# A fused attention and two-layer kernel: weight decoding without GpSimd, the mask as a TensorE product, two token blocks side by side

## The chip, the cores and the metric

One core of one Trainium2 chip runs the kernel. The metric is the device time of one execution in microseconds, as the median of three runs: 1027.07 us before (1027.04 to 1027.49). The profiled execution has a span of 1026.5 us.

## What is computed

```python
# q, k, v: [4, 8, 576, 64]; x: 2304 tokens of 512
scores = q @ k^T / 8
# heads 0-3: 0 <= i - j < 32; heads 4-7: 0 <= i - j < 128 and (i - j) % 4 == 0
attn = softmax(where(mask, scores, -1e9)) @ v      # sums + 1e-9
x  = tokens of attn, heads side by side
xn = x / sqrt(mean(x * x) + 1e-6) * rms_g
x  = (silu(xn @ w_gate) * (xn @ w_val)) @ w_out    # 512 -> 1536 -> 512
h  = x @ w_in                                      # 512 -> 2048
out = (max(h, 0) + alpha * min(h, 0)) @ w_out2     # 2048 -> 512
```

The weights arrive as float64.

## The kernel before, in words

**Blocks and layers.** The 2304 tokens make seven blocks: 0 and 1 of 256 (the first 128 tokens of two sequences each), 2 to 5 of 384, 6 of 256. Two layers work on a block: A (gate, value and out; 12 columns of 128 hidden numbers) and B (in, PReLU and out; 16 columns). A column of A is 24 first products into an accumulator of PSUM (`mm1`, L865: hi times hi, hi times lo, lo times hi, four times, for gate and for value; in the trace `psw<-xy,wb`), tanh on ScalarE, two VectorE products, a high half on ScalarE and a low one on GpSimd (`lo`, L880), and then three second products per 128 tokens into `acc` (`mm2`, L892). `mm3` and `mm4` do the same for B. Every operand is a pair of float16 numbers, high and low. `y_out` makes B's input of A's sums, `o_out` the output.

**Weights.** A block of weights is 512 numbers a partition: 12 x 3 of A, 32 of B, 68 in all. `load_w` brings the bits, `decode_w` (L197) makes float32 of them: three steps on VectorE (L202 to L204) and one add on GpSimd (L205). `norm_w` measures them: for gate and value by products of a block with itself on TensorE (`gram`, L245, and `gram_w1`, L260), a largest entry, a diagonal that TensorE spreads over the partitions (`over_partitions`, L306, L310) and `root_scale`. That is done once for each chunk of columns in `CH = [3, 9]`: no block of a chunk is scaled before all of the chunk are decoded. `split_w` (L378) makes the halves, the high one on ScalarE; the low one on VectorE (L387), or for every third block of A and every second of B by a ScalarE copy (L384) and a GpSimd subtraction (L385).

**Attention.** A step scores a group of up to 128 queries. The first 19 groups are float32 products (`f_turn`, `f_score`, `f_turn_p`, `f_value`), transposed by TensorE (L595, L621), the later 33 float16 pairs. `softmax` (L534) takes scores from PSUM, scales and masks them on VectorE by a minimum with a mask tile (L541), finds the maxima and lets ScalarE do exponentials. `a_norm` (L691, L693) divides by the root mean square, `a_xT` (L705) transposes x into a block's `xy`.

**Order.** The program issues the work of a slot (a column of a layer and block): due attention steps (`take`), decoding (`pump`), splits, first products, then second products of an earlier column (`flush`). The layers come in the order A0 A1 A2 B0 B1 B2 A3 B3 A4 B4 A5 B5, with A6 ahead of B5. In A0 all second products come after the twelve columns (`LAG0 = 12`). `N0 = 8` blocks of weights are decoded during block 0's attention; the rest of A by the end of A0, and B's during A1 and A2. A scheduler then sets the order of each engine's queue, in which the engine runs it. PSUM's eight banks are three for `acc` (`ps_a`) and five for all else (`ps_w`, in the trace `psw`). `L92` is the helper that records every product.

Of the kernel before, what the change touches and what calls it, by code (L numbers as in the profile page):

```python
# [19 lines left out]
NEG = -1.0e9  # L20
BIG = 3.0e38
# [8 lines left out]
def kernel(  # L30
# [27 lines left out]
    NXY = 3  # L58
# [4 lines left out]
    ps_a = ctx.enter_context(tc.tile_pool(name="ps_a", bufs=3, space=PSUM))  # L63
    ps_w = ctx.enter_context(tc.tile_pool(name="ps_w", bufs=5, space=PSUM))
    dram = ctx.enter_context(tc.tile_pool(name="dram", bufs=1, space=DRAM))

# [5 lines left out]
    xy = [const.tile([128, 2, KD, TMAX], F16, name=f"xy{i}") for i in range(NXY)]  # L72
# [5 lines left out]
    eps = const.tile([128, 3], BF16, name="eps")  # L78
    mhalf = const.tile([128, 1], F32, name="mhalf")
    m_norm = const.tile([96, 128], BF16, name="m_norm")  # L80
    m_tail = const.tile([32, 96], BF16, name="m_tail")
    m_spp = const.tile([128, 128], BF16, name="m_spp")
# [42 lines left out]
    def constants():  # L125
# [5 lines left out]
        nc.vector.memset(ones_1, 1.0)  # L131
        nc.vector.memset(eps, 1e-30)
        nc.gpsimd.memset(qkhl, 0.0)
        nc.vector.memset(mhalf, -0.5)
        for m in (m_spp, m_norm, m_tail):
            nc.vector.memset(m, BIG)
        band(m_spp, 128, 128, 0, -31, 0)
        # m_spd: 0 <= p - c and p % 4 == c % 4
# [8 lines left out]
        nc.vector.tensor_scalar(m_spd, same, BIG, NEG, ALU.mult, ALU.add)  # L147
        band(m_spd, 128, 128, 0, -127, 0)
        band(m_norm, 96, 128, 0, 1, 32)
# [9 lines left out]
    # A block (512 numbers a partition) is two slots of 2 KB as it comes, one as float32 and  # L159
    # one as hi | lo.  # L160
# [12 lines left out]
    def one_slot():  # L173
        # the one that has been free for the longest
# [22 lines left out]
    def decode_w(b):  # L197
# [6 lines left out]
        nc.vector.tensor_scalar(r[:, :, 0], r[:, :, 0], 29, None, ALU.logical_shift_right)  # L204
        nc.gpsimd.tensor_tensor(w, w, r[:, :, 0], ALU.add)  # L205
# [39 lines left out]
    def gram(blocks, sums, dst):  # L245
        # blocks of [k, f]: each one's own columns, or the sums over all of them
# [35 lines left out]
    def norm_w(b):  # L282
# [7 lines left out]
        else:  # L290
            # sums of squares, on the engine that waits least then
# [3 lines left out]
            if b == NBLK - 1:  # L295
# [3 lines left out]
                mm(g[:, 0:2], ones_1, eps[:, 0:2], True, False)  # L299
# [6 lines left out]
    def over_partitions(src, n, dst):  # L306
        # the largest of the partitions' src[:, i], on every partition
# [7 lines left out]
    def root_scale(p, sg, rc):  # L315
        # p: bounds of squares. sg = 2^n with sqrt(p) sg < 2^15; rc = 1 / sg
# [6 lines left out]
    # scales: gate and val of each chunk, out of each, in2, out2  # L323
# [9 lines left out]
    def scale_g():  # L333
        # sx with |x / rms * g| sx < 2^15, as |x / rms| <= sqrt(512)
# [8 lines left out]
    def scale_wo():  # L343
        # S with |out| S / (gate's scale * val's) < 2^15 in every chunk
# [12 lines left out]
        # what the last products carry: 2^-60 / (1/sx^2 * 1/S * 1/si * 1/sp)  # L357
# [33 lines left out]
    # The first 128 tokens of the sequences, the next 384 of each, and what is left of them.  # L391
# [61 lines left out]
    # the groups up to this one are float32 products  # L453
# [32 lines left out]
    def a_split_hi(i):  # L486
# [4 lines left out]
        mm(ps[:, 0:3], ones_1, eps, True, False)  # L491
# [4 lines left out]
        # sc: 0:3 the scales of q, k, v; 3:6 their inverses by 2^50; 6 that of the scores  # L496
# [36 lines left out]

    def softmax(g, scores, scale):  # L534
        # scores: (in PSUM, their heads); leaves exp(s - max) in g["s"] and its sums in g["dn"]
        nq, nk = g["nq"], g["nk"]
        s = g["s"]
        sv = s[:nq, :, :nk]
# [29 lines left out]
    # The first 128 tokens of the sequences: float32 products, as the tensor engine waits for  # L568
    # weights then; the tiles are slots of the weights that are not yet there.
# [34 lines left out]
    def f_score(i):  # L604
        g = groups[i]
        nq, nk, qk = g["nq"], g["nk"], g["qk"]
        # products of different rows of the array go to different banks
        pss = [psw()[:, 0:256].rearrange("p (h c) -> p h c", h=2) for _ in range(2)]
        for h in range(HH):
            p0 = 64 * (h % 2)  # L610
            mm(pss[h % 2][:nq, h // 2, :nk], qk[p0:p0 + 64, h // 2, :nq], qk[p0:p0 + 64, 2 + h // 2, :nk], True, True)
# [26 lines left out]
    def a_score(i):  # L638
# [3 lines left out]
        ps = psw().rearrange("p (h c) -> p h c", h=HH)  # L642
# [496 lines left out]
```

## Time and profile before

| | us |
|---|---|
| median of three runs (1027.04 to 1027.49) | 1027.07 |
| span of the profiled execution | 1026.5 |
| TensorE busy (6270 products) | 937.2, 91% |
| VectorE busy (1396 instructions) | 575.6, 56% |
| ScalarE busy (1604) | 559.9, 55% |
| GpSimd busy (394) | 377.8, 37% |

Shares are of the span of the profiled execution. The page cuts the span into 40 slices of 25.7 us; digits are tenths of a slice that the engine was busy, and PEclk the TensorE clock that was granted, in tenths of 2.4 GHz:

```profile
PE   5454879988889989999999999999999999999997
DVE  5999986787888766564445575434352111331111
POOL 3564645345534454533232333322142211122222
PEclk9676889999899999999999999999999999999999
```

PE is TensorE, PEld its loading of the stationary operand, DVE VectorE, ACT ScalarE, POOL GpSimd, SP SyncE.

### The profile page before, as it was taken

To read this page: it belongs to the slowest core of one execution; us is meant where nothing else is said; L and a number is where in the kernel's file an instruction comes from. 1 tells how busy PE (TensorE), PEld (TensorE's weight loads), DVE (VectorE), ACT (ScalarE), POOL (GpSimd) and SP (SyncE) were. 2 spreads that over 40 slices of the span, in tenths; PEclk is the share of its full clock that TensorE was granted. 3 is DMA by queue.
4 is the path that set the end of the run, shared out by engine and by line. 5 is a ranking of instruction groups with operands and counts; after the bars stand their busy time and mean duration, and the time that the engine had idled before them with its cause. 6 is when DMAs were issued, how large, how long until landed. Compare 5 with 4: busy or idle time off the path is not lost.

```text
span 1026.5 us, 17830 instructions
## 1 busy us (share of the span) xinstructions
PE 937.2 (91%) x6270; PEld 583.3 (57%) x6270; DVE 575.6 (56%) x1396; ACT 559.9 (55%) x1604; POOL 377.8 (37%) x394
## 2 busy tenths in 40 slices
PE   5454879988889989999999999999999999999997
PEld 3444765566545656665555555555555555765564
DVE  5999986787888766564445575434352111331111
ACT  3142657554669988777655677644454312333343
POOL 3564645345534454533232333322142211122222
PEclk9676889999899999999999999999999999999999
DMA  9991323643454354344344353331120000101000
GB/s 255 299 338 45 101 72 102 160 118 102 146 110 96 64 96 93 80 97 99 67 106 64 85 117 80 79 84 38 38 43 6 29 16 1 32 1 21 1 31 21
DMA packets 191608, 88.06 MB, mean 86 GB/s; under 512 B 176800, under 2 KB 180384, under 8 KB 191520
## 3 DMA queue, kind: packets, MB, share of 16 engines
q1 hardware_dynamic: 188896, 82.22, 33.0%
q10 hardware_dynamic: 2624, 4.72, 1.4%
q8 instruction: 49, 0.80, 0.3%
q14 instruction: 39, 0.32, 0.1%
HBM read 55.32 MB, written 6.55 MB: 60 GB/s over the span
## 4 chain that ended last, share of the span: by engine, by line
PE 68%; DVE 18%; DMA 6%; ACT 4%; issue 2%; POOL 1%; SPq 1%; ACTq 0%; DVEq 0%; POOLq 0%
PE psw L92 40%; PE acc L92 27%; DVE wb L203 3%; DVE wb L204 3%; DVE wb L202 2%; DMA wb<-in_moe_w_in_dram 2%; DVE wb L387 2%; DMA wb<-in_moe_w_out_dram 1%; DVE wb L693 1%; DVE wb L541 1%; DMA rkv<-in_v_dram 1%; DMA qkT<-qkhl 1%; DVE dn L556 1%; ACT wb L549 1%; POOL wb L205 1%
## 5 line engine op out<-in xcount | busy, mean ns | idle before, releaser
L92 PE MATMUL psw<-xy,wb 128*128 128x384 f16 (+1 forms) x3360 | 530.3, 307 | 5.2 <-DVE t L875 2.7
L92 PEld LDWEIGHTS <-wb 128*128 128x128 f16 (+1 forms) x4014 | 390.4, 100 | 247.5 <-issue 13.4
L92 PE MATMUL acc<-wb,hl 128*128 128x512 f16 x1002 | 246.2, 381 | 4.9 <-ACT hl L877 1.2
L932 DVE SCALAR_TENSOR_TENSOR p<-m,nal,p 128x384 f32<-128x384 f32 (+1 forms) x112 | 71.4, 638 | 166.6 <-ACT p L931 166.0
L92 PEld LDWEIGHTS <-hl 128*128 128x128 f16 x1002 | 96.0, 98 | 98.8 <-issue 3.4
L205 POOL TENSOR_TENSOR wb<-wb 128x512 int32<-128x512 int32 x68 | 100.3, 1482 | 94.5 <-DVE wb L203 61.8
L92 PE MATMUL acc<-wb 128*128 128x512 f16 x510 | 124.0, 379 | 0.7 <-ACT wb L934 0.6
L883 POOL TENSOR_TENSOR hl<-p,hl 128x384 f16<-128x384 f32 (+1 forms) x74 | 61.3, 828 | 116.4 <-ACT hl L934 103.9
L883 POOL TENSOR_TENSOR hl<-t,hl 128x384 f16<-128x384 f32 (+1 forms) x56 | 51.1, 912 | 129.6 <-ACT hl L877 129.6
L874 DVE SCALAR_TENSOR_TENSOR t<-t,psw 128x384 f32<-128x384 f32 (+1 forms) x84 | 41.2, 490 | 79.9 <-ACT t L873 79.7
L930 ACT ACTIVATE m<-psw 128x384 f32<-128x384 f32 (+1 forms) x112 | 48.6, 434 | 65.9 <-PE psw L92 65.1
L873 ACT ACTIVATE t<-psw,tsc 128x384 f32<-128x384 f32 (+1 forms) x84 | 44.1, 525 | 71.9 <-PE psw L92 62.7
L92 PE MATMUL psw<-wb 128*128 128x128 bf16 (+6 forms) x448 | 57.3, 301 | 10.7 <-POOL wb L205 8.4
L659 POOL TENSOR_TENSOR phl<-s,phl 96x512 f16<-96x512 f32 (+2 forms) x33 | 36.8, 1114 | 70.0 <-ACT phl L653 40.5
L382 ACT ACTIVATE wb<-wb,wsg 128x512 f16<-128x512 f32 x68 | 46.6, 711 | 27.3 <-DVE wrc L321 18.7
L875 DVE SCALAR_TENSOR_TENSOR t<-t,psw 128x384 f32<-128x384 f32 (+1 forms) x84 | 41.2, 490 | 27.8 <-PE psw L92 26.5
L549 ACT ACTIVATE s<-s,mx 96x128 f32<-96x128 f32 (+2 forms) x132 | 50.1, 381 | 10.9 <-DVE mx L546 10.7
L883 POOL TENSOR_TENSOR wb<-p,wb 128x384 f16<-128x384 f32 (+1 forms) x38 | 32.0, 842 | 63.5 <-ACT wb L934 57.5
L203 DVE SCALAR_TENSOR_TENSOR wb<-wb 128x512 int32<-128x512 int32 x68 | 54.7, 810 | 0.2
L883 POOL TENSOR_TENSOR wb<-t,wb 128x256 f16<-128x256 f32 (+1 forms) x28 | 24.1, 861 | 80.2 <-ACT wb L877 72.1
L877 ACT ACTIVATE hl<-t 128x384 f16<-128x384 f32 (+1 forms) x56 | 26.8, 479 | 44.4 <-DVE t L875 44.4
L934 ACT ACTIVATE hl<-p 128x384 f16<-128x384 f32 (+1 forms) x74 | 34.6, 467 | 28.9 <-DVE p L932 28.8
(160 smaller groups left out, 1154.2 us busy)
## 6 DMA issues: line engine op xcount, KB each, us to landing
wb<-in_moe_w_out_dram SPq DMA_DIRECT2D x28, 512.0 KB, 4.4
wb<-in_moe_w_in_dram SPq DMA_DIRECT2D x16, 512.0 KB, 3.6
wb<-in_moe_w_gate_dram SPq DMA_DIRECT2D x12, 512.0 KB, 7.7
wb<-in_moe_w_val_dram SPq DMA_DIRECT2D x12, 512.0 KB, 7.3
out_dram<-o ACTq DMA_DIRECT2D x16, 256.0 KB, 2.5
rkv<-in_k_dram SPq DMA_DIRECT2D x23, 128.0 KB, 2.7
rkv<-in_v_dram SPq DMA_DIRECT2D x23, 128.0 KB, 2.8
rq<-in_q_dram SPq DMA_DIRECT2D x23, 96.0 KB, 2.1
```

The lines of the kernel that those rows point to most:

```text
L92: nc.tensor.matmul(o, a, b, start=start, stop=stop)
L203: nc.vector.scalar_tensor_tensor(w, r[:, :, 1], -0x40000000, w, ALU.bitwise_and, ALU.bitwise_or)
L205: nc.gpsimd.tensor_tensor(w, w, r[:, :, 0], ALU.add)
L382: nc.scalar.activation(half(b, 0), dec(b), ACTF.Copy, scale=wsg[:, s:s + 1])
L549: nc.scalar.activation(s[:nq, h, :nk], s[:nq, h, :nk], ACTF.Exp, bias=mx[:nq, 1, h:h + 1], accum_out=g["dn"][:nq, h])
L659: nc.gpsimd.tensor_tensor(phl[:nq, 1, :, :nk], g["s"][:nq, :, :nk], phl[:nq, 0, :, :nk], ALU.subtract)
L873: nc.scalar.activation(t[:, :T], pg[:, :T], ACTF.Tanh, scale=tsc[:, chunk(c):chunk(c) + 1])
L874: nc.vector.scalar_tensor_tensor(t[:, :T], t[:, :T], 1.0, pg[:, :T], ALU.add, ALU.mult)
L875: nc.vector.scalar_tensor_tensor(t[:, :T], t[:, :T], 2.0 ** -46, pv[:, :T], ALU.mult, ALU.mult)
L883: nc.gpsimd.tensor_tensor(a[:, 1, :T], t[:, :T], a[:, 0, :T], ALU.subtract)
L930: nc.scalar.activation(m[:, :T], ps[:, :T], ACTF.Relu, scale=-(2.0 ** -15))
L932: nc.vector.scalar_tensor_tensor(p[:, :T], m[:, :T], nal[:, c:c + 1], p[:, :T], ALU.mult, ALU.add)
```

## The change

- Decoding ends on VectorE: the add becomes a shift and an or in one instruction (two inputs); GpSimd has no part in it.
- All low halves of weights are made on VectorE.
- The mask (0 or -1e38, in bfloat16) is a product: the identity times the mask, the first into the bank of the scores. VectorE's minimum goes; maxima and exponentials read PSUM.
- `CH` is `[2, 3, 3, 4]`, `N0` is 4.
- A0 and A1 alternate by column, block 1 two columns behind; both blocks' second products stand behind all of the first ones. Then come A2, A3, B0 and B1 alternating, B2, A4, B3, A5, B4, A6, B5, B6. B's weights are decoded in A2 and A3, 1.75 blocks a slot, the rest ahead of B0.
- x of blocks 0, 1 and 4 share one buffer, 2 and 5, 3 and 6 one each.
- One pool of eight banks in place of three and five.

```diff
-        nc.vector.tensor_scalar(r[:, :, 0], r[:, :, 0], 29, None, ALU.logical_shift_right)
-        nc.gpsimd.tensor_tensor(w, w, r[:, :, 0], ALU.add)
+        nc.vector.scalar_tensor_tensor(w, r[:, :, 0], 29, w, ALU.logical_shift_right, ALU.bitwise_or)
...
-    CH = [3, 9]
+    CH = [2, 3, 3, 4]
...
-        if n_split[0] % (LO1 if b < NW1 else LO2) == 0:
-            nc.scalar.activation(dec(b), dec(b), ACTF.Copy, scale=wsg[:, s:s + 1])
-            nc.gpsimd.tensor_tensor(half(b, 1), dec(b), half(b, 0), ALU.subtract)
-        else:
-            nc.vector.scalar_tensor_tensor(half(b, 1), dec(b), wsg[:, s:s + 1], half(b, 0), ALU.mult, ALU.subtract)
+        nc.vector.scalar_tensor_tensor(half(b, 1), dec(b), wsg[:, s:s + 1], half(b, 0), ALU.mult, ALU.subtract)
...
+    def masked(g, ps, n):
+        nq, nk = g["nq"], g["nk"]
+        mm(ps[:nq, 0:n, :nk], identb[:nq, :nq],
+           g["mask"][:nq, :nk].unsqueeze(1).to_broadcast([nq, n, nk]), True, False)
...
         for ps, hs in scores:
-            n = len(range(HH)[hs])
-            nc.vector.scalar_tensor_tensor(
-                s[:nq, hs, :nk], ps[:nq, :, :nk], scale,
-                g["mask"][:nq, :nk].unsqueeze(1).to_broadcast([nq, n, nk]), ALU.mult, ALU.min)
+            nc.vector.tensor_reduce(mx[:nq, 0, hs], ps[:nq, :, :nk], axis=AX.X, op=ALU.max)
+        nc.vector.tensor_scalar(mx[:nq, 1], mx[:nq, 0], scale, -1.0, ALU.mult, ALU.mult)
...
-    LAG0 = 12
-    N0 = 8
+    SKEW = 2
+    N0 = 4
...
+    for c in range(C1 + SKEW):
+        slots += [("A", j, c - SKEW * j) for j in (0, 1) if 0 <= c - SKEW * j < C1]
+    for p, j in (("A", 2), ("A", 3), ("B", 0), ("B", 2), ("A", 4), ("B", 3), ("A", 5), ("B", 4), ("A", 6), ("B", 5), ("B", 6)):
+        if (p, j) == ("B", 0):
+            slots += [("B", i, c) for c in range(C2) for i in (0, 1)]
...
+        if kind == "A" and j < 2:
+            if last and j == 1:
+                flush("A", 0, 0)
+                flush("A", 1, 0)
+        else:
+            flush(kind, j, 0 if last else LAG)
```

TensorE's queue before, from the first scale's diagonal to the first layer product (`psw<-xy`; 128x64 products are attention values, those of L705 transposes of x):

```order
L92 LDWEIGHTS ones_79
L92 MATMUL psw<-diag,ones_79 128x256
L92 MATMUL psw<-wb 128x64 x8
L705 MATMUL psw<-ident,wb 128x128 x8
L595 MATMUL psw<-ident,wb 128x128 x8
L92 LDWEIGHTS wb
L92 MATMUL psw<-xy_73,wb 128x256
```

The same place in the change (L623 are transposes of attention weights, L708 those of x; 128x128 products of `wb` behind a load are gram products, 15 more of which and the diagonal follow):

```order
L623 MATMUL psw<-ident,wb 128x128 x13
L96 MATMUL psw<-wb 128x64 x4
L623 MATMUL psw<-ident,wb 128x128 x3
L96 MATMUL psw<-wb 128x64 x12
L708 MATMUL psw<-ident,wb 128x128 x8
L96 LDWEIGHTS wb
L96 MATMUL psw<-wb 128x128
```

The value products and the transposes have moved from behind the diagonal to ahead of the gram products.

VectorE's queue before, around the second tile's normalization (L693):

```order
L691 TENSOR_SCALAR ms<-ms 128x1
L256 TENSOR_REDUCE nrm<-psw 128x1
L203 SCALAR_TENSOR_TENSOR wb<-wb 128x512
L256 TENSOR_REDUCE nrm<-psw 128x1
L310 TENSOR_SCALAR diag<-ident,nrm 128x128
L202 TENSOR_SCALAR wb<-wb 128x512
L204 TENSOR_SCALAR wb<-wb 128x512
L363 TENSOR_REDUCE big<-al 128x1
L373 TENSOR_SCALAR nal<-al 128x16
L693 SCALAR_TENSOR_TENSOR wb<-wb,ms,gs 128x512
```

In the change, around the first (L696; L208 to L210 are the decoding):

```order
L694 TENSOR_SCALAR ms<-ms 128x1
L561 TENSOR_TENSOR wb<-psw,dn 128x256
L209 SCALAR_TENSOR_TENSOR wb<-wb 128x512
L363 TENSOR_SCALAR k_101<-xsc 128x1
L208 TENSOR_SCALAR wb<-wb 128x512
L696 SCALAR_TENSOR_TENSOR wb<-wb,ms,gs 128x512
L210 SCALAR_TENSOR_TENSOR wb<-wb 128x512
```

No reduction of a gram product (L256) and no diagonal (L310) stands ahead of the normalization any more; decoding steps still do.

## Rows read from the trace of the kernel before

**Rows 1.** Stretches: span, busy time of PE, PEld, DVE, ACT, POOL; PEclk, DMA share, GB/s.

```profile
0.00:63.50 63.50, 28.10 (x138) 21.80 (x139) 52.07 (x119) 19.50 (x55) 31.77 (x38) 0.78 1.00 293
63.50:269.00 205.50, 167.23 (x1231) 123.48 (x1230) 176.96 (x372) 108.44 (x326) 105.47 (x87) 0.88 0.40 119
269.00:430.00 161.00, 151.62 (x1101) 95.03 (x1100) 117.91 (x293) 133.71 (x392) 75.67 (x80) 1.00 0.45 92
430.00:1026.40 596.40, 590.20 (x3805) 342.96 (x3803) 228.63 (x615) 298.24 (x831) 164.86 (x191) 1.00 0.23 50
```

**Rows 2.** Chain of waits, 840 to 1026: start us, us, engine, tile, line, count.

```profile
844.43 3.90 PE psw L92 x24
848.33 1.94 PE acc L92 x9
...
888.57 2.29 PE psw L92 x21
892.49 2.29 PE psw L92 x21
```

**Rows 3.** Two stretches, first products (tile xy): PE, DVE, ACT, clock, DMA.

```profile
63.50:269.00 205.50, 86.52 (x594) 4.23 (x7) 3.12 (x6) 0.88 0.40 119
269.00:430.00 161.00, 90.79 (x613) 0.00 (x0) 0.00 (x0) 1.00 0.45 92
```

**Rows 4.** The same stretches, second products (tile acc).

```profile
63.50:269.00 205.50, 34.82 (x138) 1.47 (x2) 2.62 (x6) 0.88 0.40 119
269.00:430.00 161.00, 66.41 (x264) 3.62 (x5) 7.83 (x17) 1.00 0.45 92
```

**Rows 5.** Stretches, VectorE's masking alone (L541): DVE, PEclk, DMA share, GB/s.

```profile
63.50:269.00 205.50, 11.53 (x30) 0.88 0.40 119
269.00:430.00 161.00, 7.10 (x10) 1.00 0.45 92
430.00:1026.40 596.40, 15.94 (x23) 1.00 0.23 50
```

**Rows 6.** PE's timeline, 25 to 64: start us, us, operation [idle before, releaser].

```profile
30.60 0.41 PE L621 MATMUL psw<-ident,wb 128*128 128x128 f32 x1
...
40.73 0.39 PE L92 MATMUL psw<-diag,ones 128*128 128x256 bf16 x1 [8.36 <-DVE diag L310]
40.91 3.56 PE L92 MATMUL psw<-wb 128*128 128x64 f32 x16
...
60.92 1.09 PE L705 MATMUL psw<-ident,wb 128*128 128x128 f32 x4 [15.59 <-DVE wb L693]
```

**Rows 7.** DVE's timeline, 44 to 64.

```profile
45.23 1.50 DVE L204 TENSOR_SCALAR wb<-wb 128x512 int32<-128x512 int32 x1
...
50.82 0.68 DVE L707 TENSOR_TENSOR xy<-psw,xy 128x512 f16<-128x512 f32 x1
...
59.13 1.64 DVE L693 SCALAR_TENSOR_TENSOR wb<-wb,ms,gs 128x512 f32<-128x512 f32 x1
```

**Rows 8.** PE's timeline, 76 to 97.

```profile
81.62 4.45 PE L92 MATMUL psw<-wb 128*128 128x128 bf16 x40 [6.16 <-POOL wb L205]
...
94.83 0.37 PE L92 MATMUL psw<-diag,ones 128*128 128x256 bf16 x1 [6.11 <-DVE diag L310]
```

**Rows 9.** Decoding by line: duration ns min/median/max, first to last start us.

```profile
L203 DVE SCALAR_TENSOR_TENSOR wb<-wb x68: 654/678/1777, 5.3 to 295.0; 128x512 int32<-128x512 int32 x68
...
L204 DVE TENSOR_SCALAR wb<-wb x68: 408/420/1498, 5.0 to 294.1; 128x512 int32<-128x512 int32 x68
...
L205 POOL TENSOR_TENSOR wb<-wb x68: 1272/1292/2961, 6.1 to 295.7; 128x512 int32<-128x512 int32 x68
```

**Rows 10.** POOL's timeline, 44 to 48.

```profile
44.72 3.15 POOL L205 TENSOR_TENSOR wb<-wb 128x512 int32<-128x512 int32 x2 [1.63 <-DVE big L365]
```

**Rows 11.** Low halves on VectorE (L387): DVE, PEclk, DMA share, GB/s.

```profile
269.00:430.00 161.00, 13.39 (x16) 1.00 0.45 92
```

**Rows 12.** Low halves on GpSimd (L385): POOL, PEclk, DMA share, GB/s.

```profile
269.00:430.00 161.00, 18.85 (x16) 1.00 0.45 92
```

More of the change, by code (lines that the diff above doesn't have):

```diff
@@ L19 @@
 EXPO = 0x7F800000
-NEG = -1.0e9
-BIG = 3.0e38
+NEG = -1.0e38
 @with_exitstack
@@ L71 @@
     wbi = wb.bitcast(I32)
-    xy = [const.tile([128, 2, KD, TMAX], F16, name=f"xy{i}") for i in range(NXY)]
+    xy0 = const.tile([128, 2 * 2 * KD * 256], F16, name="xy0")
+    xyl = [const.tile([128, 2, KD, TMAX], F16, name=f"xy{i}") for i in (1, 2)]
+    xy = [xy0[:, i * 2 * KD * 256:(i + 1) * 2 * KD * 256].rearrange("p (a k t) -> p a k t", a=2, k=KD) for i in range(2)]
+    xy += xyl + [xy0[:, 0:2 * KD * TMAX].rearrange("p (a k t) -> p a k t", a=2, k=KD)] + xyl
+    after_b = {4: (0, 1), 5: (2,), 6: (3,)}
     gs = const.tile([128, DM], F32, name="gs")
@@ L146, in constants @@
         mm(same, et.rearrange("p a c -> p (a c)"), et.rearrange("p a c -> p (a c)"), True, True)
-        nc.vector.tensor_scalar(m_spd, same, BIG, NEG, ALU.mult, ALU.add)
+        nc.vector.tensor_scalar(m_spd, same, -NEG, NEG, ALU.mult, ALU.add)
         band(m_spd, 128, 128, 0, -127, 0)
-        band(m_norm, 96, 128, 0, 1, 32)
+        band(m_band, 128, 160, 0, 1, 32)
         for r in range(2):
@@ L830, in hl_take @@
         T = ncols(j % 100)
-        if j == 0:
-            h_at[c] = one_slot()
-            t = wb16[:, h_at[c] * 1024:h_at[c] * 1024 + 2 * T].rearrange("p (a t) -> p a t", a=2)
+        if j < 2:
+            if c not in h_at:
+                h_at[c] = [one_slot(), 2]
+            o = h_at[c][0] * 1024 + j * 512
+            t = wb16[:, o:o + 2 * T].rearrange("p (a t) -> p a t", a=2)
         else:
@@ L844, in hl_give @@
         t = ah_at.pop((j, c))
-        if j == 0 and c in h_at:
-            give(h_at.pop(c))
+        if j < 2:
+            h_at[c][1] -= 1
+            if h_at[c][1] == 0:
+                give(h_at[c][0])
         else:
@@ L887, in accumulate @@
             if first:
-                acc[n] = ps_a.tile([128, DM], F32, tag="acc", name="acc")
+                acc[j, n] = ps_w.tile([128, DM], F32, tag="w", name="acc")
             for u, (l, m) in enumerate(((0, 0), (0, 1), (1, 0))):
-                mm(acc[n], a[:, l, n * 128:(n + 1) * 128], half(b, m), first and u == 0, last and u == 2)
+                mm(acc[j, n], a[:, l, n * 128:(n + 1) * 128], half(b, m), first and u == 0, last and u == 2)
     def mm2(j, c):
@@ L946, in o_out @@
             o = wk.tile([128, DM], F32, tag="st", bufs=2, name="o")
-            nc.scalar.activation(o, acc[n], ACTF.Copy, scale=rc[:, n:n + 1])
+            nc.scalar.activation(o, acc[j, n], ACTF.Copy, scale=rc[:, n:n + 1])
             col = 0
@@ L957 @@
     LAG = 1
-    LAG0 = 12
-    N0 = 8
+    SKEW = 2
+    N0 = 4
     START = (-1, 0, 1, -1, 2, -1, 3, -1)
     RAW = 10
-    PUMP = (1.5, 1.5, 2.0)
-    SP0, SP1 = 10, 6
-    LOOK = 4
-    phases = [(p, j) for p in "AB" for j in range(3)]
-    for j in range(3, NJ - 2):
-        phases += [("A", j), ("B", j)]
-    phases += [("A", NJ - 2), ("A", NJ - 1), ("B", NJ - 2), ("B", NJ - 1)]
-    ahead = {j + 1 for n, (p, j) in enumerate(phases) if p == "A" and phases[n + 1:n + 3] == [("B", j), ("A", j + 1)]}
-    slots = []
-    for p, j in phases:
-        slots += [(p, j, c) for c in range(C1 if p == "A" else C2)][LOOK if p == "A" and j in ahead else 0:]
-        if p == "A" and j + 1 in ahead:
-            slots += [("A", j + 1, c) for c in range(LOOK)]
+    PUMP = 1.75
+    slots = []
+    for c in range(C1 + SKEW):
[4 more added lines that the diff above has]
+        else:
+            slots += [(p, j, c) for c in range(C1 if p == "A" else C2)]
     def dur(s):
@@ L986 @@
     need = [(n + 1, start_of[j] - 8.0) for n, (_, j) in enumerate(steps) if j]
+    steps_of = {j: n + 1 for n, (_, j) in enumerate(steps) if j is not None}
     done_b = set()
-    state = dict(done=0, clock=0.0, credit=0.0, spare=12)
+    state = dict(done=0, clock=0.0, credit=0.0, pump=0.0, spare=6)
     def take(d):
@@ L994, in take @@
         got = []
-        while steps and state["credit"] >= 1.0 and len(got) < 2:
+        while steps and state["credit"] >= 1.0 and len(got) < 3:
             j = steps[0][1]
-            if j is not None and j >= NXY and j - NXY not in done_b:
+            if j is not None and not done_b.issuperset(after_b.get(j, ())):
                 break
@@ L1004, in first_step @@
     def first_step():
-        steps.popleft()[0]()
+        f, j = steps.popleft()
+        assert j is None or done_b.issuperset(after_b.get(j, ()))
+        f()
         state["done"] += 1
@@ L1034, in pump_to @@
             pump(1)
+            assert loaded or n_done[0] >= n, (n_done, n, sum(free), len(later))
     pend = {}
@@ L1078 @@
             f()
+        while kind == "A" and state["done"] < steps_of[j]:
+            first_step()
         if (kind, j) == ("A", 0):
@@ L1082 @@
                 split_w(b)
-        if kind == "A" and j < 3:
-            state["spare"] = (SP0, SP1, 3)[j]
-            state["pump"] = state.get("pump", 0.0) + PUMP[j]
+        if kind == "A" and j in (2, 3):
+            state["spare"] = 6 if j == 2 else 3
+            state["pump"] += PUMP
             pump(int(state["pump"]))
             state["pump"] -= int(state["pump"])
-        while (kind, j, c) == ("B", 0, 0) and (loaded or later):
-            pump(1)
+        if (kind, j, c) == ("B", 0, 0):
+            state["spare"] = 2
+            pump_to(NBLK)
         if (kind, j) == ("B", 0):
@@ L1100 @@
         last = c == (C1 if kind == "A" else C2) - 1
-        early_one = kind == "A" and j in ahead and c < LOOK
-        flush(kind, j, 0 if last else LAG0 if (kind, j) == ("A", 0) else LOOK if early_one else LAG)
+        if kind == "A" and j < 2:
+            if last and j == 1:
+                flush("A", 0, 0)
+                flush("A", 1, 0)
+        else:
+            flush(kind, j, 0 if last else LAG)
 _INS = ['q', 'k', 'v', 'moe_w_gate', 'moe_w_val', 'moe_w_out', 'moe_rms_g', 'moe2_w_in', 'moe2_w_out', 'moe2_alpha']
```

65 lines of the change are left out of this document (32 added, 33 removed).

## The prediction, made before the changed kernel ran

> **What bounds the kernel now.** I read the cut into stretches first, then the chain of waits, then TensorE's timeline where it stands. The four stretches [rows 1] end where the first layer product starts (63.5 us), where blocks 0 and 1 are through the first layer but for a few products (269), and where as many products are done as the change has before its block 0 enters the second layer (430). After 430 TensorE is busy for 590.2 of 596.4 us at full clock: there it is the bound. Before 269 it is busy for 28.1 of 63.5 and 167.2 of 205.5 us, at a granted clock of 0.78 and 0.88 of 2.4 GHz, while VectorE is busy for 52.1 and 177.0: the loss sits there.
>
> The layer products have a fixed price at full clock [rows 2]: 24 of 384 columns take 3.90 us, nine of 512 take 1.94 (0.216 each), and one column of a 256 block takes 892.49 - 888.57 = 3.92, of which six of 512 are 1.29 and 24 of 256 the other 2.63 (0.110 each). A block of 384 costs 12 x (3.90 + 1.94) + 16 x (3.90 / 2 + 1.94) = 132.3, one of 256 costs 12 x 3.92 + 16 x (2.63 / 2 + 1.29) = 88.6; four and three of them make **795 us**, in either kernel. The other 231 us of the span of 1026.5 are attention, scales, waiting and slow clock. By stretch:
> - 0 to 63.5: no layer product.
> - 63.5 to 269 (205.5): 594 products of mostly 256 columns [rows 3] and 138 of 512 [rows 4], some 95 us; idle 205.5 - 167.2 = 38; the clock's missing 12% of the busy time, 20; so attention and scales 52, for 15 groups (30 mask instructions, two for a group there [rows 5]).
> - 269 to 430 (161): idle 9.4; 613 products [rows 3], by the program 270 of them with 384 columns, and 264 of 512 [rows 4] make 270 x 0.1625 + 343 x 0.110 + 264 x 0.216 = 138.6, I take 139; so 12.6 for ten groups, 1.26 each.
> - 430 to the end (596.4): products 795 - 95 - 139 = 561; idle 6.2; 29 for 23 groups [rows 5], again 1.26 each.
>
> **The change, part by part.** *Start.* The first product waits for x of block 0. The last transpose of the attention weights ends at 31.0, but TensorE then does gram products and stands 8.36 us at the diagonal of their scale, with 16 value products queued behind it; and it stands 15.59 us for the second tile's normalization on VectorE, whose queue is full of decoding [rows 6]. In the change the value products and the transposes stand ahead of most gram products, and four decodes instead of eight are asked for first. The values can then start at 31 and take 3.6 [rows 6]; normalization is, for each of two tiles, 1.64 for the scaling and 0.68 for each of two copies [rows 7], 1.09 for transposes [rows 6] and about 0.4 for the square's sum, 4.5: 9 in all, so 44. Gram, diagonal, scale and first splits come to 4 more: **48**. Bounds: 43 if these lie wholly beside that, 58 if the second tile waits as long as 10 us.
>
> *Blocks 0 and 1 in the first layer* (the change has their attention and first products side by side). Products 95, attention and scales of the same 15 groups 52, two groups more 2.5, and 30 mask products: by the rate above 0.11 each, so 3; the nearest row for one that starts alone is 0.37 [rows 8], so at most 11, and a gain is excluded, as they are added to TensorE. That is 152. What is lost besides? Before, 38 + 20 = 58. The largest piece is the second chunk of nine columns: between 75 and 95 TensorE waits 6.16 and 6.11 us [rows 8] for 18 decodes and then for their scale. With chunks of 2, 3, 3 and 4 columns the wait is cut in pieces, between which the second block's products stand; I keep three scale chains of 6 us (18), 10 for the second block's attention, which now comes due as early as the first columns, and 5 at half clock. Bounds: 10, and all 58. 152 + 33 = 185, so **233** instead of 269.
>
> Is VectorE the bound there? A decode now is 0.42 + 0.68 + 0.68 us there (medians [rows 9]) instead of 0.42 + 0.68 + 0.42 and a GpSimd add of 1.29. But VectorE's instructions are held up: a single-input step of 0.42 takes 1.50 [rows 7] beside a GpSimd add that runs from 44.72 [rows 10]. Pricing the stretch's 372 VectorE instructions at the shortest common duration of their forms (as 0.42 and 0.68) gives 127 us, against 177.0 busy [rows 1]: 50 more, beside 105.5 us of GpSimd, 0.47 for each. For the change the same count is 117, beside 16 us of GpSimd: 117 + 7 = 124 of 185. Not the bound.
>
> *Blocks 2 and 3, with the second layer's weights.* The change decodes 30 blocks here instead of 6, and VectorE takes the low halves of all 27 splits, where of 32 it had 16 [rows 11] and ScalarE and GpSimd 16 [rows 12]; 15 groups run instead of ten. TensorE: products 140, 15 groups at 1.26, 19, and a 512-column mask product for each at 0.216, 3: 162. VectorE: the count is 85 before, against 117.9 busy beside 75.7 of GpSimd [rows 1], 0.44 for each. In the change it is 139. GpSimd loses six adds (7.7) and 18.9 of splits [rows 12], which leaves 49, and five groups' subtractions come on top, some 52: 139 + 0.44 x 52 = 162. Two engines equally full cannot hide each other: I give 16 us of idle TensorE instead of 9.4. 178, so **411** instead of 430. Nothing hides VectorE's work here: if it is late, the splits are, and TensorE waits. Bounds: 165 (3 of idle) and 188.
>
> *From there.* Products 795 - 95 - 140 = 560, 16 groups instead of 23 at 1.26 and 0.216 for the mask, 24, idle 6.2: 590 instead of 596.4. The eight-bank pool I cost at nothing: in this stretch TensorE's 6.2 us of idle are all that banks could cost, and where blocks 0 and 1 sum in four banks, four are left for the products; at worst that doubles the 6. ScalarE loses 28 copies; with 133.7 busy of 161 [rows 1] it has no more to do. 48 + 185 + 178 + 590 = 1001, and with the 0.6 us around the span (the median is 1027.07, the profiled span 1026.5) **1002 us**.
>
> **The rivals.** *VectorE bounds blocks 2 and 3* (slower). If each of GpSimd's 52 us cost VectorE a whole one, it needs 139 + 52 = 191; and if it then reaches only the share of its busiest long stretch, 177.0 of 205.5 or 86% [rows 1], the stretch is 222 and the kernel 1002 + 44 = 1046. It decides once VectorE needs over 176: the stretch then passes 205, and the kernel 1029. The rows before come to 0.44 and 0.47 of that price. For: all decoding and all low halves stand in one queue. Against: most of GpSimd's share is gone. Chance 0.13.
> The Trainium skill, "SBUF — State Buffer", section "Who interferes with whom", says that a VectorE instruction with two SBUF inputs, or in a two-port mode, and one of GpSimd exclude each other, the second waiting for the whole of the first. By that rule the price could be this rival's; the 1.50 us step agrees with it, the averages bear out half.
> *The waits only move.* The side-by-side blocks wait for the same weights and lose 45 to 58, not 33; with masks at 0.37 the stretch is at most 152 + 8 + 58 = 218, the kernel 1002 + 33 = 1035, and 1014 to 1027 with cheap masks. For: TensorE's queue has a fixed order, and four scale chains in it instead of two. Against: each chain has other products ahead of it. Chance 0.12.
> *It packs.* Start at 44, losses of 10, third stretch 165: 1002 - 4 - 23 - 13 = 962. For: at each chain TensorE has another block's products. Against: VectorE is 162 of the 165. Chance 0.13.
> That the change doesn't do what it says its order excludes: no add on GpSimd and no mask on VectorE is left.
>
> **How the numbers follow.** The forecast has 0.62 and, with its bounds partly used, 975 to 1024. The range of 970 to 1030 leaves out most of the packed case and of VectorE's, and the end of the moved waits. A difference under 0.2% (2 us) can't be told from none. Faster: 0.61 of the forecast, 0.13 packed, 0.04 of the moved waits: 0.78. Same: 0.01, 0.05 of the moved waits and 0.01 of VectorE's: 0.07. Slower: 0.03 and 0.12: 0.15.
>
> **What would show it.** The first layer product at 43 to 58; blocks 0 and 1 through the first layer near 233, block 0's entry into the second layer near 411; decode steps at their medians, with none over 1 us except beside a GpSimd subtraction; idle TensorE between these two marks 3 to 26 us. I am wrong if TensorE idles for more than 60 us between the first product and 411, if its last 590 us change, or if the mask products cost more than 15 us together.

## The result, and the profile after

The change made the kernel **slower: 1036.86 us** (median of four runs, 1035.23 to 1038.1) against 1027.05 (four runs), 1.0% by these medians; the ratio that goes with the runs is 1.0104 (95% interval 1.0087 to 1.0122). The prediction was 1002, 970 to 1030. The profiled execution has a span of 1035.7 us, 9.2 more than before.

The stretches of the change, cut at the same work as [rows 1] (first layer product; blocks 0 and 1 through layer A; as many products as stand ahead of B0; the end), with the same columns:

```profile
0.00:53.50 53.50, 31.95 (x143) 23.88 (x143) 33.11 (x97) 17.09 (x56) 7.49 (x19) 1.00 1.06 287
53.50:232.90 179.40, 159.75 (x1290) 120.39 (x1291) 143.68 (x382) 103.39 (x329) 31.53 (x32) 0.90 0.46 124
232.90:424.90 192.00, 170.14 (x1158) 97.06 (x1157) 154.10 (x407) 142.76 (x413) 56.53 (x51) 0.96 0.58 134
424.90:1035.70 610.80, 590.18 (x3756) 346.88 (x3754) 197.26 (x509) 290.33 (x780) 161.98 (x195) 0.99 0.19 40
```

| stretch | before | predicted | after |
|---|---|---|---|
| to the first layer product | 63.5 | 48 | 53.5 |
| blocks 0 and 1 in layer A | 205.5 | 185 | 179.4 |
| the products of A2 and A3, or as many | 161 | 178 | 192.0 |
| the rest | 596.4 | 590 | 610.8 |

Up to 233 us the numbers came as forecast and 36 us were won. Then 31 were lost in 192 us, 17 of them forecast: TensorE idles there for 192.0 - 170.1 = 21.9 us, and is busy for 170.1 us at a granted clock of 0.96 where 162 were forecast. Another 14 were lost in the rest, where TensorE now idles for 610.8 - 590.2 = 20.6 us instead of 6.2.

TensorE's timeline at the start (start, us, operation, idle time before it and its releaser), for [rows 6]:

```profile
36.91 1.12 PE L708 MATMUL psw<-ident,wb 128*128 128x128 f32 x4 [2.24 <-DVE wb L696]
40.14 1.09 PE L708 MATMUL psw<-ident,wb 128*128 128x128 f32 x4 [2.11 <-DVE wb L696]
...
47.93 0.37 PE L96 MATMUL psw<-diag,ones 128*128 128x256 bf16 x1 [5.00 <-DVE diag L315]
...
53.49 0.28 PE L96 MATMUL psw<-xy,wb 128*128 128x256 f16 x1 [2.63 <-ACT wb L383]
```

The 15.59 us for the second tile are 2.11, and x is transposed at 41.2, ahead of the sum's 44. From there to the first layer product it takes 12.3 us where the sum had 4: the diagonal still costs 5.00 and a split 2.63. Runs whose edits lie behind blocks 0 and 1 reach the first layer product at 50.3 to 54.5, so that some 3 us of the difference are not the change's own. The last step of decoding, for [rows 9] (ns min/median/max, first to last start):

```profile
L210 DVE SCALAR_TENSOR_TENSOR wb<-wb x68: 649/680/1518, 5.8 to 338.1; 128x512 int32<-128x512 int32 x68
```

Decoding ends at 338 us instead of 296: the second layer's weights moved to where A2 runs.

### The profile page after: what moved, and what is told of

It reads as the page before. It is cut to its first block, busy times and chain, and to the rows that moved or that the text cites. A ratio compares the mean times of both kernels' runs of the same rounds, so it can differ in the third digit from the quotient of the medians.

```text
span 1035.7 us, 17720 instructions
## 1 busy us (share of the span) xinstructions
PE 952.0 (92%) x6343; PEld 588.2 (57%) x6343; DVE 528.2 (51%) x1391; ACT 553.6 (53%) x1576; POOL 257.5 (25%) x296
## 4 chain that ended last, share of the span: by engine, by line
PE 61%; DVE 11%; DMA 6%; ACT 5%; issue 3%; SPq 1%; POOL 1%; ACTq 0%; DVEq 0%; POOLq 0%
PE psw L96 35%; PE acc L96 25%; DVE wb L209 2%; DMA qkT<-qkhl 1%; DVE wb L210 1%; DMA rkv<-in_k_dram 1%; ACT s L548 1%; DVE wb L208 1%; DMA rq<-in_q_dram 1%; DMA xy<-yhl 1%; DVE t L882 1%; DVE mx L543 1%; DVE t L883 1%; DVE wb L384 1%; DMA pT<-phl 1%
## 5 line engine op out<-in xcount | busy, mean ns | idle before, releaser
L96 PE MATMUL psw<-xy,wb 128*128 128x384 f16 (+1 forms) x3360 | 518.7, 305 | 4.4 <-ACT wb L383 2.6
L96 PEld LDWEIGHTS <-wb 128*128 128x128 f16 (+1 forms) x3975 | 382.5, 99 | 232.0 <-issue 10.8
L96 PE MATMUL acc<-wb,hl 128*128 128x512 f16 x1041 | 258.3, 387 | 19.8 <-ACT hl L942 11.3
L96 PE MATMUL acc<-wb 128*128 128x512 f16 x471 | 113.7, 385 | 5.0 <-ACT wb L383 3.1
L891 POOL TENSOR_TENSOR hl<-p,hl 128x384 f16<-128x384 f32 (+1 forms) x84 | 67.6, 805 | 168.8 <-ACT hl L942 161.2
L891 POOL TENSOR_TENSOR wb<-t,wb 128x256 f16<-128x256 f32 (+1 forms) x36 | 32.8, 911 | 164.5 <-ACT wb L885 154.3
L548 ACT ACTIVATE s<-psw,mx,sc 96x128 f32<-96x128 f32 (+2 forms) x132 | 56.8, 435 | 12.1 <-DVE mx L544 8.3
L384 DVE SCALAR_TENSOR_TENSOR wb<-wb,wsg 128x512 f16<-128x512 f32 x68 | 51.7, 782 | 4.2 <-ACT wb L383 3.4
L939 ACT ACTIVATE p<-psw 128x384 f32<-128x384 f32 (+1 forms) x112 | 49.0, 437 | 0.0
L210 DVE SCALAR_TENSOR_TENSOR wb<-wb 128x512 int32<-128x512 int32 x68 | 47.9, 714 | 0.2
L209 DVE SCALAR_TENSOR_TENSOR wb<-wb 128x512 int32<-128x512 int32 x68 | 47.0, 701 | 0.2
```

The costliest lines, as they stand in the source:

```text
L96: nc.tensor.matmul(o, a, b, start=start, stop=stop)
L209: nc.vector.scalar_tensor_tensor(w, r[:, :, 1], -0x40000000, w, ALU.bitwise_and, ALU.bitwise_or)
L210: nc.vector.scalar_tensor_tensor(w, r[:, :, 0], 29, w, ALU.logical_shift_right, ALU.bitwise_or)
L548: nc.scalar.activation(s[:nq, h, :nk], ps[:nq, n, :nk], ACTF.Exp, bias=mx[:nq, 1, h:h + 1], scale=scale, accum_out=g["dn"][:nq, h])
L891: nc.gpsimd.tensor_tensor(a[:, 1, :T], t[:, :T], a[:, 0, :T], ALU.subtract)
L939: nc.scalar.activation(p[:, :T], ps[:, :T], ACTF.Relu, scale=2.0 ** -15)
```

## The experiments

Labels that begin with b_ are the kernel before with parts of the change, a_ the change with parts undone. The first theory put the loss on the order of the blocks (attention held back until B0 and B1 are done), the rival on the parts.

### Parts put into the kernel before

**b_no_gpsimd** (decoding and low halves).

```diff
-        nc.vector.tensor_scalar(r[:, :, 0], r[:, :, 0], 29, None, ALU.logical_shift_right)
-        nc.gpsimd.tensor_tensor(w, w, r[:, :, 0], ALU.add)
+        nc.vector.scalar_tensor_tensor(w, r[:, :, 0], 29, w, ALU.logical_shift_right, ALU.bitwise_or)
...
-        if n_split[0] % (LO1 if b < NW1 else LO2) == 0:
-            nc.scalar.activation(dec(b), dec(b), ACTF.Copy, scale=wsg[:, s:s + 1])
-            nc.gpsimd.tensor_tensor(half(b, 1), dec(b), half(b, 0), ALU.subtract)
-        else:
-            nc.vector.scalar_tensor_tensor(half(b, 1), dec(b), wsg[:, s:s + 1], half(b, 0), ALU.mult, ALU.subtract)
+        nc.vector.scalar_tensor_tensor(half(b, 1), dec(b), wsg[:, s:s + 1], half(b, 0), ALU.mult, ALU.subtract)
```

> The kernel before, with two parts of the change: the last step of decoding and all low halves of weights on VectorE, GpSimd in neither. Theory O (the order of the blocks costs the time: attention of block 4 is held until both B0 and B1 are done and then comes in a bunch): these two parts are good by themselves, since the 118 us of GpSimd adds and subtractions that go had cost VectorE 0.45 us each, 53, against some 40 us of added VectorE work: 1010 to 1022 us. Theory P (the parts cost it, not the order): VectorE, full from 25 to 130 us, gets more work: 1030 to 1045.

**b_decode_dve** (the first hunk of that diff alone).

> The kernel before with the last step of decoding on VectorE alone, low halves as before. If each us of GpSimd costs VectorE 0.45 us until 270, the 100 us of adds that go give 45 back and 68 instructions of 0.68 for 0.42 take 18: some 27 of the 37 us: 996 to 1005. If the low halves were the larger part: 1010 to 1022.

Measured: **989.37 us**, ratio 0.9641 (0.9626 to 0.9655), more than either theory gave, and 990.94 for decoding alone. The first two stretches of b_no_gpsimd, cut at the same work:

```profile
0.00:53.20 53.20, 28.01 (x139) 21.77 (x139) 40.33 (x111) 18.40 (x53) 8.37 (x21) 0.86 1.02 283
53.20:234.50 181.30, 156.23 (x1228) 118.90 (x1227) 162.79 (x392) 101.08 (x314) 26.29 (x29) 0.90 0.49 153
```

Blocks 0 and 1 are through at 234.5 us **in the old order, with the old chunks and masks**; the whole change needs 232.9. So taking GpSimd out is worth the whole gain up to there; what the chunks and the order do besides cancels, as the runs below show. The same step undone inside the change gives it back, **a_add_on_gpsimd** (the first hunk the other way round):

> The changed kernel with the last step of decoding back on GpSimd. In the kernel before, this part alone was worth 35 us, until 235 us of the span. If the parts add: 1060 to 1078 us, and the first layer of blocks 0 and 1 ends near 265 instead of 233. If blocks side by side hide GpSimd's adds: 1036 to 1050.

1075.63 us, 38.8 above the change: this part adds, as expected. But blocks 0 and 1 end at 248 us, not near 265, and 22 of the 38.8 stand in block 2 (112.7 us instead of 90.9), where the second layer's weights are now decoded.

**b_mask** (the `masked` products and the new `softmax`, as in the diff of the change, alone) and **b_one_pool**:

```diff
-    ps_a = ctx.enter_context(tc.tile_pool(name="ps_a", bufs=3, space=PSUM))
-    ps_w = ctx.enter_context(tc.tile_pool(name="ps_w", bufs=5, space=PSUM))
+    ps_w = ctx.enter_context(tc.tile_pool(name="ps_w", bufs=8, space=PSUM))
...
-                acc[n] = ps_a.tile([128, DM], F32, tag="acc", name="acc")
+                acc[n] = ps_w.tile([128, DM], F32, tag="w", name="acc")
```

> The kernel before with the mask as a product alone. Theory O: VectorE loses 37.6 us of masking, of which a part lay on the way before 270, TensorE gets 71 products of 0.1 to 0.35 us; 1018 to 1030 us. Theory P: a product that heads every score and exponentials that hold a bank of PSUM for longer: 1032 to 1042.

> The kernel before with one pool of eight banks alone. Theory O: nothing, 1024 to 1030 us, as TensorE idles for 6 us in all after 430. Theory P: sums and products that take each other's banks make TensorE wait behind ScalarE's and VectorE's reading: 1032 or more, with idle time in the last 600 us.

1034.07 us, ratio 1.0085 (1.0065 to 1.0104), and 1036.48, 1.0107 (1.009 to 1.0124): both are losses by themselves, 8 and 10 us. For the mask, one stretch of equal products (200 to 600 us of them) before:

```profile
431.50:824.90 393.40, 392.92 (x2555) 221.58 (x2554) 184.61 (x509) 230.19 (x673) 123.30 (x137) 1.00 0.32 69
```

and with it:

```profile
428.40:829.10 400.70, 398.42 (x2583) 224.46 (x2582) 170.78 (x486) 235.39 (x673) 123.36 (x137) 1.00 0.33 67
```

The stretch grew by 7.3 us. TensorE has 5.5 more to do for 23 groups, 0.24 each, and VectorE 13.8 less, which nobody waits for there; ahead of the stretch 3.1 are won (428.4 against 431.5). Why one pool costs is open: in its profiled run, the fastest of the four, the loss is spread, 1.5 us ahead of 433 and 2.6 from there to 829.

**b_no_gpsimd_chunks**, which is b_no_gpsimd with

```diff
-    CH = [3, 9]
+    CH = [2, 3, 3, 4]
...
-    N0 = 8
+    N0 = 4
```

and **all_but_order**, the same with the edits of b_mask and b_one_pool too.

> The kernel before with decoding and low halves on VectorE and the chunks of 2, 3, 3 and 4 (four blocks decoded first). The parts measured so far add up to 1007 without the chunks, against 1012 with them: if parts add, the chunks are worth -3 to +7: 986 to 997 us. If they save the waits for the nine-column chunk, as the prediction had it: 970 to 982.

> The kernel before with decoding and low halves on VectorE, mask as a product, chunks of 2, 3, 3 and 4 and one pool, in the old order of blocks: all of the change but the order. Theory S: 989 + 8 + 10 = 1007, with the chunks unknown within 6: 1000 to 1014 us, 10 groups of attention done between the end of layer A for blocks 0 and 1 and the point of 234.6 us of products, in 160 to 170 us instead of 192. Theory I: 1025 to 1040.

1002.48 us, so the chunks **lose 13** where the prediction counted on them, and 1012.43: mask and pool together cost 10 here, not 18, so these two do not add. In b_no_gpsimd_chunks TensorE meets the last chunk's gram products in the middle of A0:

```profile
138.46 1.87 PE L92 MATMUL psw<-wb 128*128 128x128 bf16 x12 [3.70 <-DVE wb L204]
143.76 1.21 PE L92 MATMUL psw<-wb 128*128 128x128 bf16 x8 [3.43 <-DVE wb L204]
```

The wait for decoding is not gone, it stands later; b_no_gpsimd has none there.

### The order behind A1

**side_by_side_only** is b_no_gpsimd_chunks with A0 and A1 side by side, **a_old_tail** is all_but_order with the same edit, which also decodes the second layer's weights in A2 alone (not shown):

```diff
-    phases = [(p, j) for p in "AB" for j in range(3)]
+    phases = [("A", 2)] + [("B", j) for j in range(3)]
...
+    for c in range(C1 + SKEW):
+        slots += [("A", j, c - SKEW * j) for j in (0, 1) if 0 <= c - SKEW * j < C1]
```

> The kernel before with decoding and low halves on VectorE, the chunks, and blocks 0 and 1 side by side in layer A, but the old order behind them (A2 B0 B1 B2 A3 B3 ...), the mask on VectorE and the old pools. Theory S: side by side is no loss, the order behind A1 is: 975 to 992 us. Theory I: side by side itself makes VectorE late: 995 to 1015.

> The changed kernel with the old order behind A1 (A2 B0 B1 B2 A3 B3 A4 B4 A5 A6 B5 B6, four columns of the next A ahead), and nothing else changed: B's weights are decoded in A2 alone. Theory S: the 30 us of the order come back but for what A2 loses to decoding: 1002 to 1018 us. Theory I: 1028 or more.

1013.16 and 1015.82 us. A0 beside A1 is no gain: it costs 10.7 us in the first pair (1002.48 without it), inside the range of the theory against it, and 3.4 in the second (1012.43 without it; the runs scatter by that much). But it does gain where the prediction looked for it. These are the times, in us, at which layer products worth 95 us (blocks 0 and 1 in layer A) and 235 us have started, each priced as in the prediction:

| layer products | b_no_gpsimd | b_no_gpsimd_chunks | side_by_side_only | all_but_order | a_old_tail | change |
|---|---|---|---|---|---|---|
| 95 us | 234.0 | 242.4 | 234.0 | 238.2 | 227.0 | 232.2 |
| 235 us | 391.6 | 403.9 | 415.8 | 400.7 | 404.3 | 424.5 |

Side by side wins 8 and 11 us up to the first mark, about what the chunks lose there, and loses 20 and 15 up to the second. Of the 68 loads of weights, 21 (side_by_side_only) and 14 (a_old_tail) come behind the first mark, instead of 4 and 5.

The order behind A1, with what goes with it (the buffers of x, one for `pT` where there were two, the pace of decoding), costs 1036.86 - 1015.82 = 21. Where? **a_a3_later** moves A3, and decodes the second layer's weights in A2 alone:

```diff
-    for p, j in (("A", 2), ("A", 3), ("B", 0), ("B", 2), ("A", 4), ("B", 3), ("A", 5), ("B", 4), ("A", 6), ("B", 5), ("B", 6)):
+    for p, j in (("A", 2), ("B", 0), ("A", 3), ("B", 2), ("A", 4), ("B", 3), ("A", 5), ("B", 4), ("A", 6), ("B", 5), ("B", 6)):
...
-    PUMP = 1.75
+    PUMP = 2.5
```

> The changed kernel with A3 behind B0 and B1, so that block 3's ten groups of attention lie beside A2, B0 and B1 instead of A2 alone, and B0 and B1 have attention beside them. B's weights are decoded at 2.5 blocks a slot in A2. Theory V: the groups leave A2 but seven more decodes enter it; some of the loss stays: 1015 to 1030. Theory L: the loss goes with the groups: 1000 to 1015.

1020.34 us: A3 ahead of B0 and B1, with the pace of decoding that goes with it, makes 16.5 of the 21. Two more runs tried attention and VectorE as causes: **a_b3_first** (in the same line `("B", 3)` ahead of `("A", 4)`) and **a_mask_dve** (the old `softmax` with its minimum, no `masked`):

> The changed kernel with B3 ahead of A4, so that block 4's attention, which may start only when B0 and B1 are done, has 124 us of products to lie beside instead of 62. Theory O: the 14 us of idle time between 496 and 600 and the low clock there go for the most part: 1018 to 1027 us. Theory P: nothing changes, 1033 to 1040.

> The changed kernel with the mask back on VectorE. Theory S (the parts add up: decoding and low halves on VectorE -37 us, mask +8, one pool +10, and the order of the blocks behind A1 costs the rest, some 30): 1024 to 1031 us, the 8 us of the mask come back, for the most part behind 425 us. Theory I (the parts cost more together than alone, VectorE being fuller): masking on VectorE again makes A2 and A3 slower, 1036 to 1048.

1040.03 and 1037.54 us, neither better. The first moved no attention (in both, 36 and 43 of the 52 groups are scored when 300 and 400 us of products are done), so it tells nothing. The second came out where masking on VectorE was expected to slow A2 and A3: the mask's price on TensorE came back, and as much was lost in A2 and A3, which end at 433 instead of 425. **a_light_decode** (the first hunk: for the second layer's weights two of the three steps are left out) asked VectorE directly, **a_small_loads** (both: of these loads an eighth is brought) then the loads:

```diff
+        if b < NW1:
             nc.vector.scalar_tensor_tensor(w, r[:, :, 1], -0x40000000, w, ALU.bitwise_and, ALU.bitwise_or)
             nc.vector.scalar_tensor_tensor(w, r[:, :, 0], 29, w, ALU.logical_shift_right, ALU.bitwise_or)
...
+            nc.sync.dma_start(out=wbi[:, i * 512:i * 512 + 128], in_=src.bitcast(I32)[:, 0:128])
```

> The changed kernel with the second layer's weights decoded in one step of three: the two steps that put in the sign and the low bits are left out for these 32 blocks, so 23 x 2 instructions of 0.72 us, 33 us of VectorE, are gone from 233 to 324 us, where VectorE is busy for 78 of 91 us. Theory V (VectorE bounds block 2's first layer there, as 23 decodes lie in it): these 91 us become 62 to 75, the kernel 1008 to 1022. Theory L (the chain of one group of attention, some 10 us for each of block 3's ten groups with one buffer for each transposed tile, bounds it): 1030 to 1038.

> As a_light_decode (the second layer's weights decoded in one step of three), and of each of their 32 loads only an eighth is brought, so some 14 MB do not come between 233 and 330 us, where the DMA engines are busy for 0.75 of the time; what is computed of these weights is not the reference's. Theory D (the loads bound A2: attention's own loads and transposes wait behind them): block 2's stretch of 91 us becomes 62 to 78, the kernel 1010 to 1024. Theory L (the chain of each group of attention, ten groups in 70 us of products): 1031 to 1039.

1036.16 and **1023.59** us (1017.57 to 1029.20, a wide scatter; 0.9969, 0.9945 to 0.9993). The same 55 us of products (block 2 in layer A) in the change, in a_light_decode, and in a_small_loads:

```profile
232.90:324.00 91.10, 73.14 (x497) 41.30 (x496) 78.55 (x211) 60.64 (x188) 29.96 (x24) 0.93 0.75 185
```

```profile
235.00:330.00 95.00, 77.57 (x520) 43.80 (x519) 54.94 (x174) 62.85 (x201) 22.57 (x24) 0.87 0.80 195
```

```profile
230.00:308.00 78.00, 69.84 (x521) 40.42 (x519) 55.14 (x173) 62.37 (x199) 21.83 (x24) 0.98 0.62 115
```

Read VectorE's time, the one with (x211) and (x174): from 78.55 to 54.94 us, and the stretch does not shrink. With an eighth of each load it shrinks by 17: 9 us of idle time, and 8 of busy time at a clock of 0.98 instead of 0.87. **The loads bound it, not VectorE.** What TensorE waits for most of its 18 idle us in the change is an attention group's transposed tile (us in all, times, longest):

```profile
PE psw L96 <- DMA qkT<-qkhl: 11.9, 5, 6.6
```

So the loads cost time beside the attention's own transfers. In a_a3_later the same layer products run beside 14 of the loads at full size and three groups of attention, instead of 17 and seven:

```profile
226.30:300.30 74.00, 63.88 (x399) 35.48 (x398) 62.21 (x153) 47.21 (x139) 21.09 (x13) 0.93 0.64 168
```

That is the whole of what a_a3_later wins. In the old order 34 of the 68 loads lie between 63.5 and 268 us, where the DMA engines are busy for 0.40 [rows 1].

**a_14col_shared, a_14col_bufs, a_14col_own_x** leave out two of the second layer's 16 columns and so gain memory; the first, the control, and the third have B0 and B1 in turn. `C2` and `NSLOT` are changed in all three runs, the buffers of `qkT` and `pT` in the second, the buffer of x in the third:

```diff
-    C2 = w_in2.shape[0]
+    C2 = w_in2.shape[0] - 2
...
-    NSLOT = 70
+    NSLOT = 66
...
-        qkT = at.tile([128, 3 * HH, 128], F16, tag="qkT", bufs=1, name="qkT")
+        qkT = at.tile([128, 3 * HH, 128], F16, tag="qkT", bufs=2, name="qkT")
-        g["pT"] = at.tile([128, 2 * HH, 128], F16, tag="pT", bufs=1, name="pT")
+        g["pT"] = at.tile([128, 2 * HH, 128], F16, tag="pT", bufs=2, name="pT")
...
-    xy += xyl + [xy0[:, 0:2 * KD * TMAX].rearrange("p (a k t) -> p a k t", a=2, k=KD)] + xyl
+    xy += xyl + [const.tile([128, 2, KD, TMAX], F16, name="xy4")] + xyl
-    after_b = {4: (0, 1), 5: (2,), 6: (3,)}
+    after_b = {5: (2,), 6: (3,)}
```

> The changed kernel without the last two columns of the second layer (14 instead of 16), which takes 2 x (4 x 3.90 + 3 x 2.62) = 47 us of products out, with four slots of weights fewer, and B0 and B1 one after the other. The control for the next two: 984 to 994 us if one after the other costs nothing.

> The changed kernel without the last two columns of the second layer, as the control, B0 and B1 side by side; the memory so gained holds a second buffer for each of the two transposed tiles of an attention group (qkT, pT). Theory L: the groups' chains overlap, the 91 us of block 2 become 72 to 82, the kernel 8 to 18 us under the control. Theory D: within 4 us of the control.

> The changed kernel without the last two columns of the second layer, B0 and B1 one after the other as in the control, and block 4's x in a buffer of its own, so that its attention need not wait for B0 and B1. Theory O for what is lost behind 425 us: TensorE's idle time around 500 to 570 goes, 8 to 16 us under the control. If that idle time has another cause: within 4 us of the control.

975.30, 988.37 and 982.22 us. The second is 13 above the control, but the control has B0 and B1 in turn and the second has not, so this alone says nothing of the buffers. The third is no gain, but the control leaves its attention nothing to gain: TensorE waits for 0.2 us in it from 425 to 620, and it came out faster than expected. **a_b_in_turn** has B0 and B1 in turn alone:

```diff
-            slots += [("B", i, c) for c in range(C2) for i in (0, 1)]
+            slots += [("B", i, c) for i in (0, 1) for c in range(C2)]
```

> The changed kernel with B0 and B1 one after the other and nothing else changed. With 14 columns the kernel with B0 and B1 in turn was 13 us faster than the one side by side with two buffers, and idled for under 1 us from 425 to 620 us instead of 8. If side by side in the second layer costs that: 1022 to 1030 us. If the buffers made the difference: 1033 to 1040.

**1022.37 us**, 14.5 faster than the change. That is about the 13 between the second run of 14 columns and its control: more buffers do not help. From 235 to 400 us of the layer products, in a_b_in_turn and in the change:

```profile
430.80:606.40 175.60, 175.60 (x1209) 108.99 (x1208) 71.43 (x197) 109.93 (x323) 55.76 (x68) 1.00 0.30 64
```

```profile
424.50:616.30 191.80, 179.77 (x1198) 108.83 (x1197) 72.41 (x196) 110.38 (x322) 55.45 (x68) 0.98 0.27 58
```

Side by side, TensorE idles for 12.0 us there, and in turn not at all. In both kernels one group of attention is scored in the first 65 us of these products and seven in the other 100, so attention is held back alike: my first theory falls. Both have the pool of eight banks.

What stands in the way there, first ScalarE's, then TensorE's timeline of the change:

```profile
516.41 1.26 ACT L918 ACTIVATE yhl<-acc,sg 128x512 f16<-128x512 f32 x2
...
521.75 0.60 ACT L915 ACTIVATE yhl<-acc 128x512 f32<-128x512 f32 x1 [0.49 <-DMA xy<-yhl]
...
522.33 0.51 ACT L942 ACTIVATE hl<-p 128x384 f16<-128x384 f32 x1
```

```profile
522.90 2.32 PE L96 MATMUL acc<-wb,hl 128*128 128x512 f16 x5 [4.07 <-ACT hl L942]
```

L915 and L918 are `y_out` of block 3. Its layer A was done by 425, but ScalarE reads its three sums for the last time at 516, 517 and 525, behind all of B0 and B1, where B2 begins. The third sum's readings wait for a buffer that a transpose still reads, and the high half for which TensorE waits 4.07 us stands behind the first of them in ScalarE's queue. With B0 and B1 in turn the last readings are at 478, 479 and 484, where B0 is done and B1 begins, and TensorE waits for nothing. Until 516 these three sums and the four of B0 and B1 hold seven of the eight banks, and yet TensorE does not wait from 445 to 512, so that it is not shown that the banks cost anything. The wait shown is the longest; waits for such high halves make 8.5 of the 12.0 us, 3.2 of them at 432 to 436, where B0 and B1 begin. What puts the readings so late in the queues is the scheduler's order; I did not try to move them alone, so that their part in the loss is argued, while the loss of B0 beside B1 is shown.

## Why the prediction was wrong, point by point

- **Start, 48:** measured 53.5, inside 43 to 58: x was ready early, and the 4 us behind it were 12.3, by the waits shown.
- **Blocks 0 and 1, 185:** 179.4, but *the step that failed is "the largest piece is the second chunk of nine columns".* The old order without GpSimd takes 181.3. The chunks lose 13 us, 8 of them up to this mark, and the side-by-side blocks win as much there and lose it again behind it. So 233 came out by luck: the forecast left out the largest gain, GpSimd's, and counted on one that is a loss. I had measured what GpSimd cost VectorE, 0.47 us for each us of GpSimd, and used it only to ask whether VectorE was the bound in the change, not to credit its removal: 100 us of adds at that price are 47, less 68 x 0.26 = 18 for the longer last step, 29; measured 35. That VectorE's time is the reason is argued and not shown: in [rows 8] TensorE waits 6.16 us for GpSimd's add itself, so the chain to a split also became shorter by an engine, and no run separates the two.
- **A2 and A3, 178 (165 to 188):** 192.0, by 21.9 us of idle time instead of 16 and 170.1 of busy time instead of 162. *The step that failed is "Nothing hides VectorE's work here", with the loads at nothing.* I moved 24 decodes and priced their VectorE time, but not the 24 loads of 512 KB that move with them and lie beside the transfers of seven groups of attention. The VectorE rival, 1029 to 1046, gave nearly the right time for the wrong engine, with this stretch over 205: a_light_decode refutes it.
- **The rest, 590:** 610.8. *The step that failed is "idle 6.2", with B0 beside B1 at nothing.* I doubled the 6 at worst; it was 20.6. I asked what B0 and B1 side by side need only of the banks, and not when block 3's sums would be read and what stands behind them in the queues. The eight-bank pool by itself is not what failed here: with it, and B0 and B1 in turn, the same rest takes 594. The masks were about right: 0.24 us a group where I took 0.216.
- **The waits that only move, 1035 at worst, chance 0.12,** was nearest in time and kind, but placed at the scale chains of blocks 0 and 1; the waits came in A2, and from the start of B0 and B1 to block 2's second layer.

By medians, each part put on top of the ones ahead of it: 1026 before, decoding -35, low halves -2, chunks +13, mask and pool +10, A0 beside A1 +3, B0 beside B1 with A3 behind them +4.5, A3 ahead of them +16.5: 1037. In another sequence the same parts cost other sums: A0 beside A1 is +10.7 ahead of mask and pool, which then make 2.7. A3 ahead of B0 has a part in both losses behind A1: with it block 2 takes 91 us instead of 74, and B0 beside B1 costs 14.5; without it the whole step that has B0 beside B1 is 4.5. The gains of a_small_loads (-12.6 against a_light_decode) and a_b_in_turn (-14.5) make 27 where the order costs 21, so they overlap, or the old order has a part of these losses too. The fastest version that computes everything is the one part that helps, b_no_gpsimd at 989.37 us, 4.6% under the change. It is open why one pool costs 10 us in the old order, and what in the side-by-side edit loses the time behind blocks 0 and 1.

## What to carry to other kernels

Credit a removal with the price that the trace already shows for what it disturbs: here GpSimd's adds went with VectorE time of about half their own, and one line was worth more than the new order. When a step moves, move its loads in the ledger too and look at the DMA share, and at the other transfers, of the place where they land. A sum that is read late puts its readings ahead of others in a queue: ask of every accumulator when it is read, not only whether there is a bank for it. A stretch that comes out as forecast can hide a gain and a loss: test its parts one by one.

## What the runs showed of the hardware

Without GpSimd's adds and subtractions of weights VectorE decoded faster: the three decode steps took 38.7 + 54.7 + 40.1 = 133 us before and 28.9 + 47.1 + 46.3 = 122 in b_no_gpsimd, although the last became longer by 68 x 0.26 = 18. The Trainium skill, "SBUF — State Buffer", section "Who interferes with whom", says that a VectorE instruction with two SBUF inputs, or in a two-port mode, and one of GpSimd exclude each other, so that one waits for the whole of the other's instruction; the averages of the prediction, 0.44 and 0.47 us of VectorE for each us of GpSimd, are about half of that. Medians don't show it: the first step takes 415 ns before and 416 in b_no_gpsimd, while the longest falls from 1529 to 904. It is the slow instructions that go.
